# Attention and a two-layer MLP on one core: loading the first units' queries without their zeros, in two half-height parts

## The chip, the cores and the metric

The kernel runs on one core of a Trainium2 chip. The metric is the device time of one execution in microseconds (us), as the median of repeated runs; a smaller time is better. One execution was also taken by the hardware profiler, and the profile and the trace of this text are from it.

## The reference

There are 4 sequences of 768 positions, 8 heads of 64 elements, and 8 memory keys and values per head. Attention is chunked: a chunk of 32 queries sees 16 positions to its left, its own 32, 8 to its right, and the memory. All is in 32-bit floats.

```python
for c in range(nc):                                   # chunks of 32
    k_full = concat(mem_k, k[l_start:r_end])          # v_full likewise
    scores = scale * q_c @ k_full.T
    a = exp(scores - max(scores))
    out[c] = (a / (sum(a) + 1e-9)) @ v_full
x = out.transpose(0, 2, 1, 3).reshape(3072, 512)
h = x @ w_in                                          # 512 -> 2048
g = maximum(h, 0) + alpha * minimum(h, 0)
result = g @ w_out                                    # 2048 -> 512
```

## The kernel before

**Units.** Attention is cut into 32 units: a half of a sequence (384 positions) times a pair of heads, the two heads' 64 elements making the 128 rows of a tile. Units 0 to 7 (two halves with four pairs each) go a way of their own, `windows` (L496), because the MLP can't start before them; the later 24 go through `scores`, `weights` and `turn`, between matmuls of the MLP.

**The first units.** What unit u needs lies in one of four tiles `early` (L212), unit u + 4 coming after unit u in the same tile. A tile has three parts: queries, keys, values. The query part has 768 columns: for each of the 12 chunks 64 columns, 32 of the one head and 32 of the other. Only the rows of a column's own head hold queries; the other 64 rows hold zeros, so that one matmul with 128 rows gives the scores of both heads. These zeros are written on the host (`qd` in `_layout`, L927) and come with the load. `load_first` (L485) issues two DMAs a unit: queries and keys in one (656 KB), values in another (256 KB).

For each of these units `windows` then plans:

- TensorE: `score_products` (L300) loads 64 columns of queries as weights and streams 64 keys through them, 12 times (24 matmuls in the trace, since a 32-bit product is issued as two). The scores stand in one of two PSUM banks, `s_ps`, by the parity of u. In units 0 to 2 a few idle matmuls stand ahead of it (`stir`, L295).
- VectorE: `top` (L502, a memset and a maximum), `less` (L511, subtract it), then ScalarE `exps`, VectorE `total` (L519) and `inverse`, GpSimd `scale` (L526, into `ew`), TensorE `turn` (L541, six transposes), ScalarE `keep`, TensorE `values` (L553), and `split` (L465), which writes the two parts `xh` and `xl` that the MLP takes.

**The MLP.** Weights come by `load_w` (L594), 512 KB a DMA, and are rebuilt on ScalarE and VectorE (`decode_part`, L613) into two parts. `up` (L718, tile `h_ps`) and `down` (L747, tile `o_ps`) are the matmuls that fill nearly all of TensorE's time. The last four weight tiles lie where the `early` tiles lay.

**The order of the work.** Every step is given to a planner (`Plan`, L123) with its engine, a cost, what it reads and writes, and a due time (`rest`). `send` (L143) plays the steps with these costs: of the steps that could run next on an engine it takes the one with the longest way behind it, and issues it. A load's consumers are ready `LAND` (2.3) after the load's cost on SP has passed; `SHIFT` adds to or takes from the priority of ten single steps, by their number in the order of planning. Each engine then runs its own list in that order. All loads are issued from SP's queue.

Of the kernel before, what the change touches and what calls it, by code (L numbers as in the profile page):

```python
# [18 lines left out]
P = 128  # L19
B, H, S, D = 4, 8, 768, 64  # L20
NM = 8
CH, LEFT, RIGHT = 32, 16, 8
# [3 lines left out]
NJ = TQ // CH  # L26
TK = LEFT + TQ + RIGHT
BT = 384
NHALF = B * S // BT
NT = BT // TQ  # L30
NPAIR = H // 2
# [36 lines left out]
NKT = TK + 2 * NM  # L68
STARTS = (0, LEFT + CH // 2, TK - 2 * CH + 2 * NM)

PE, DVE, ACT, POOL, SP = "PE", "DVE", "ACT", "POOL", "SP"

HOP, LAND, FOLLOW = 0.07, 2.3, 0.1

# [31 lines left out]
NWIN, NSET = 2 * NPAIR, 4  # L108

STARTS_WIN = (0, 2 * LEFT, NKT - KW)  # L110
NQ = NT * NJ * 2 * CH
NV = NT * 2 * D
# [4 lines left out]
GATHER_ACT, HIGH_ACT = range(2, 14), 24  # L117


SHIFT = {5: -7.5, 7: -3.1, 9: -1.3, 10: 4.5, 11: 6.7, 64: 3.3, 65: -2.4, 80: -3.2, 113: -3.6, 172: 8.5}  # L120


class Plan:  # L123
# [19 lines left out]
    def send(self):  # L143
# [6 lines left out]
        for n in reversed(range(len(self.steps))):  # L150
            engine, cost, _, _, rest = self.steps[n]
            behind[n] = max(rest, cost + max((behind[m] + lag[engine] for m in users[n]), default=0.0))
        for n, more in SHIFT.items():
            behind[n] += more
# [27 lines left out]
def body(ctx: ExitStack, tc: tile.TileContext, qvw, kw, first, w_in, w_out, alpha, out):  # L182
    nc = tc.nc
# [22 lines left out]
    qk = [const.tile([P, BT + NT * NKT], F32, name=f"qk{i}") for i in range(NKB)]  # L206
# [4 lines left out]

    early = [wps[NF - NSET + i, 0].tile([P, NQ + NT * NKT + NV], F32, name="early", tag="w") for i in range(NSET)]  # L212
    ews = [turned.tile([P, 2, NJ, P], F32, name=f"ew{i}", tag=f"pt{i}") for i in range(NPT)]
    nc.gpsimd.memset(eye, 0.0)
    nc.gpsimd.affine_select(out=eye, in_=eye, compare_op=ALU.not_equal, fill=1.0, base=0, pattern=[[-1, P]],
                            channel_multiplier=1)
# [11 lines left out]
    step = plan.add  # L228
# [20 lines left out]
    def rest(place):  # L249
        wide = NNARROW * NF  # L250
        return (len(ORDER) - max(place, wide)) * WIDE_PAIR + max(wide - place, 0) * PAIR

    def begins(u):

        return u // NPAIR if u < NWIN else BEGIN[(u - NWIN) // 2]

    def due(u, later=0):

        return rest(begins(u) + later + (5.5 if u >= FIRST_FRONT else 0))
# [35 lines left out]
    def stir(t, num):  # L295

        for _ in range(num):
            nc.tensor.matmul(out=t, lhsT=busy[:, :P], rhs=busy, start=True, stop=True)

    def score_products(u):  # L300
        blk, pr = divmod(u, NPAIR)
        st = state[u]
        s_ps = ps_s.tile([P, 512], F32, name="s_ps", tag=f"s{u % 2}")
        stir(s_ps, STIR[0] if u == 0 else STIR[1] if u < 3 else STIR[2])
        st["s"] = s_ps[:, :2 * NJ * KW].rearrange("p (n k) -> p n k", k=KW)
        t = early[u % NSET]
        q = t[:, :NQ].rearrange("p (c x) -> p c x", c=NT * NJ)
        keys = t[:, NQ:NQ + NT * NKT].rearrange("p (t k) -> p t k", t=NT)
        for n in range(2 * NJ):
            for i in range(2):  # L310
                t, j = n // NJ * 2 + i, n % NJ
                nc.tensor.matmul(  # L312
                    out=st["s"][i * 2 * CH:(i + 1) * 2 * CH, n],
                    lhsT=q[:, t * NJ + j],
                    rhs=keys[:, t, STARTS_WIN[j]:STARTS_WIN[j] + KW],
                    start=True, stop=True,
                )
# [167 lines left out]
    def load_first(u):  # L485
        blk, pr = divmod(u, NPAIR)
        t = early[u % NSET]

        def load(lo, hi):
            nc.sync.dma_start(out=t[:, lo:hi], in_=first[blk, pr, :, lo:hi])  # L490

        state[u] = {}
        step(SP, 1.6, partial(load, 0, NQ + NT * NKT), writes=[("qk", u % NSET)], rest=due(u))
        step(SP, 0.78, partial(load, NQ + NT * NKT, NQ + NT * NKT + NV), writes=[("fv", u % NSET)], rest=due(u))

    def windows(u):  # L496

        st = state[u]
        sk, tks, ak = ("s", u % 2), [("o", 0), ("o", 1)], ("o", 2) if u % 2 else "a"
# [53 lines left out]
        def values():  # L553
# [3 lines left out]
            for t in range(NT):  # L557
                for h2 in range(2):
# [4 lines left out]
                        start=True, stop=True,  # L563
                    )

        step(PE, 1.33 if u < 3 else 0.8, partial(score_products, u), reads=[("qk", u % NSET)], writes=[sk], rest=due(u))
        step(DVE, 0.66, top, writes=[sk, ("mx", u % 3)])
        step(DVE, 0.55, less, reads=[sk, ("mx", u % 3)], writes=e_keys(u))
        step(ACT, 0.52, exps, writes=e_keys(u))
# [24 lines left out]
    def load_w(f):  # L594
        def load(i):
            k, j = ((f, i), 0) if f < NAPART else ((f, 0), i)
            if k not in raw:
                raw[k] = wps[k].tile([P, 2 if f >= NAPART else 1, DM, 2], I32, name="w_t", tag="w")
            nc.sync.dma_start(out=raw[k][:, j].rearrange("p m b -> p (m b)"), in_=srcs[i][f])  # L599

        i = f - NF + NSET
        after = [("qk", i), ("fv", i)] if i >= 0 else []
        for i in range(2):
            step(SP, 1.31, partial(load, i), writes=[("r", f, i)] + after, rest=rest(place_of(f)))

    def place_of(f):
        return PLACE[0, f]
# [229 lines left out]
    def unit_begins(u):  # L837
        if u < NWIN:
            windows(u)
        else:  # L840
            if u % 2 == 0:
                scores([u, u + 1])
        if u < NWIN and u + NSET < NWIN:
            load_first(u + NSET)
        elif u >= NWIN - NKB and u + NKB < NU:
            load_unit(u + NKB)

    for u in range(NSET):
        load_first(u)
        if u == 1:  # L850
            step(SP, 0.6, partial(nc.sync.dma_start, out=al, in_=alpha), writes=["al"])
            step(DVE, 0.1, partial(nc.vector.tensor_scalar, out=rise, in0=al, scalar1=-1.0, scalar2=1.0, op0=ALU.mult,
                                    op1=ALU.add), reads=["al"], writes=["rise"])
    for f in range(NF - NSET):
        load_w(f)
# [3 lines left out]
    for f in range(NF - NSET, NF):  # L859
        load_w(f)  # L860
# [49 lines left out]
def _layout(q, k, v, mem_k, mem_v, moe_w_in, moe_w_out, moe_alpha):  # L910
    import numpy as np

    nh = S // BT
    qT = q.reshape(B, NPAIR, 2, nh, BT, D).transpose(0, 3, 1, 2, 5, 4)
    pad = ((0, 0), (0, 0), (LEFT, RIGHT), (0, 0))
    kp, vp = np.pad(k, pad), np.pad(v, pad)

    def keys(x, mem, s, *spans):
        return np.concatenate([mem if p is None else x[:, :, s + LEFT + p[0]:s + LEFT + p[1]] for p in spans], axis=2)

    kwin = np.stack([keys(kp, mem_k, t * TQ, (-16, 16), None, (16, 72), None, (72, 104)) for t in range(S // TQ)],
                    axis=2)
    kwin = kwin.reshape(B, NPAIR, 2, nh, NT, NKT, D).transpose(0, 3, 1, 2, 6, 4, 5)
    vwin = np.stack([keys(vp, mem_v, t * TQ, (-16, 16), None, (16, 104)) for t in range(S // TQ)], axis=2)
    vwin = vwin.reshape(B, NPAIR, 2, nh, NT, P, D).transpose(0, 3, 1, 5, 4, 2, 6)
    nwin = NWIN // NPAIR
    qd = np.zeros((nwin, NPAIR, 2, D, NT * NJ, 2, CH), q.dtype)  # L927
    for h in range(2):
        qd[:, :, h, :, :, h] = qT.reshape(NHALF, NPAIR, 2, D, NT * NJ, CH)[:nwin, :, h]
    kfirst = np.stack([keys(kp, mem_k, t * TQ, (-16, 16), None, (16, 104), None) for t in range(S // TQ)], axis=2)  # L930
    kfirst = kfirst.reshape(B, NPAIR, 2, nh, NT, NKT, D).transpose(0, 3, 1, 2, 6, 4, 5)
    kfirst = kfirst.reshape(NHALF, NPAIR, P, NT * NKT)[:nwin]
    vparts = vwin.reshape(NHALF, NPAIR, P, NV)
    return dict(
        qvw=np.concatenate([qT.reshape(NHALF, NPAIR, P, BT), vparts], axis=3),
        kw=np.ascontiguousarray(kwin).reshape(NHALF, NPAIR, P, NT, NKT),
        first=np.concatenate([qd.reshape(nwin, NPAIR, P, NQ), kfirst, vparts[:nwin]], axis=3),
        w_in=np.ascontiguousarray(moe_w_in.reshape(NK, P, NF, P).transpose(2, 1, 0, 3)
                                  ).reshape(NF, P, NK * P).view(np.int64),
        w_out=np.ascontiguousarray(moe_w_out.reshape(NF, P, DM)).view(np.int64),  # L940
        alpha=np.ascontiguousarray(moe_alpha.reshape(NF, P).T),
    )
# [15 lines left out]
```

## Time and profile before

| | |
|---|---|
| median of 3 runs | 598.65 us (598.43 to 599.91) |
| the profiled execution | 598.74 us |
| its span, first to last instruction | 596.8 us |
| TensorE matmul busy | 588.1 us (99%) |
| VectorE busy | 387.1 us (65%) |
| ScalarE busy | 210.9 us (35%) |
| GpSimd busy | 37.9 us (6%) |
| mean granted TensorE clock | 1.000 |

In the profile PE is TensorE's matmuls, PEld its weight loads, DVE VectorE, ACT ScalarE, POOL GpSimd, and SPq the queue of SyncE, which issues DMAs. Times in the views are us from the first instruction. A row of the timeline gives start, busy time, engine, line, operation, the written and the read tiles, the shape and a count; in square brackets stands the idle time ahead of it and what ended it. The chain is the work that ended last, followed back from the last instruction. A time between the span and the execution's 598.74 us lies around the program, outside the views.

### The profile page before, as it was taken

How to read it: one execution, taken by the hardware profiler on the slowest of the kernel's cores; microseconds unless marked ns; L12 is line 12 of the kernel's file. 1: busy time of each engine (PE TensorE's matmuls, PEld its weight loads, DVE VectorE, ACT ScalarE, POOL GpSimd, SP SyncE). 2: the span in 40 equal slices, each digit the busy share in tenths (PEclk: the TensorE clock that was granted, in tenths of full speed). 3: DMA queues.
4: the chain of work that ended last, by engine and by line, in shares of the span. 5: the costliest groups of instructions: out<-in, count | busy, mean ns of one | idle time of the engine just before them, and what ended most of it. 6: DMA issues, size and time to landing. Idle time of an engine off the chain costs nothing.

```text
span 596.8 us, 10948 instructions
## 1 busy us (share of the span) xinstructions
PE 588.1 (99%) x4412; PEld 504.9 (85%) x4412; DVE 387.1 (65%) x904; ACT 210.9 (35%) x580; POOL 37.9 (6%) x61
## 2 busy tenths in 40 slices
PE   7999999999999999999999999999999999999997
PEld 4789989888998989989898888888888888888886
DVE  5888889887958768695895852861862771530530
ACT  3788887635122504423233302302400411210201
POOL 3510000010001101010010100100100100000000
PEclk9999999999999999999999999999999999999999
DMA  8999600222040312503304003003101000000001
GB/s 328 351 400 407 246 0 1 66 65 89 2 153 2 100 33 69 152 3 100 100 1 154 1 1 100 2 0 112 60 1 36 0 1 36 36 1 0 1 1 70
DMA packets 21075, 48.95 MB, mean 82 GB/s; under 512 B 2464, under 2 KB 5792, under 8 KB 21024
## 3 DMA queue, kind: packets, MB, share of 16 engines
q1 hardware_dynamic: 20880, 48.12, 22.8%
q8 instruction: 34, 0.56, 0.4%
q14 instruction: 17, 0.14, 0.1%
q10 hardware_dynamic: 144, 0.13, 0.1%
HBM read 41.95 MB, written 6.29 MB: 81 GB/s over the span
## 4 chain that ended last, share of the span: by engine, by line
PE 96%; DMA 3%; SPq 0%; ACT 0%; issue 0%; ACTq 0%
PE h_ps L723 45%; PE o_ps L753 44%; PE a_ps L438 3%; DMA early<-first 3%; PE s_ps L337 2%; PE a_ps L559 1%; PE o_ps L546 0%; PE s_ps L312 0%; SPq L490 0%; SPq L599 0%; ACT o_t L810 0%; ACTq L810 0%
## 5 line engine op out<-in xcount | busy, mean ns | idle before, releaser
L723 PE MATMUL h_ps<-xh,w 128*128 128x384 f32 (+1 forms) x896 | 248.7, 358 | 0.0
L723 PEld LDWEIGHTS h_ps<-xh,w 128*128 128x128 f32 x896 | 164.9, 188 | 16.0
L753 PE MATMUL o_ps<-w,gh 128*128 128x512 f32 x528 | 162.7, 389 | 0.0
L723 PE MATMUL h_ps<-xl,w 128*128 128x384 f32 (+1 forms) x448 | 162.6, 363 | 0.0
L732 ACT ACTIVATE g<-h_ps 128x384 f32<-128x384 f32 (+1 forms) x112 | 60.4, 540 | 195.3 <-PE h_ps L723 129.8
L735 DVE SCALAR_TENSOR_TENSOR g<-g,rise,h_ps 128x384 f32<-128x384 f32 (+1 forms) x112 | 74.7, 668 | 74.8 <-ACT g L732 74.1
L753 PEld LDWEIGHTS o_ps<-w,gh 128*128 128x128 f32 x528 | 99.1, 188 | 20.5
L413 DVE STREAM_TRANSPOSE pt<-e 32x64 f32<-32x64 f32 (+1 forms) x336 | 99.3, 300 | 7.4 <-POOL e L392 2.0
L753 PE MATMUL o_ps<-w,gl 128*128 128x512 f32 x264 | 102.8, 389 | 0.0
L723 PEld LDWEIGHTS h_ps<-xl,w 128*128 128x128 f32 x448 | 84.1, 188 | 10.2
L753 PE MATMUL o_ps<-w,xh 128*128 128x512 f32 x240 | 74.8, 393 | 0.0
L753 PEld LDWEIGHTS o_ps<-w,gl 128*128 128x128 f32 x264 | 49.6, 188 | 10.2
L477 DVE TENSOR_TENSOR xl<-a_ps,xh 128x384 fp32r<-128x384 f32 x32 | 17.6, 552 | 59.7 <-ACT xh L474 59.0
L753 PEld LDWEIGHTS o_ps<-w,xh 128*128 128x128 f32 x240 | 45.0, 188 | 8.9
L392 POOL TENSOR_TENSOR e<-e,den 128x384 f32<-128x384 f32 x24 | 22.8, 948 | 419.6 <-DVE den L389 270.0
L474 ACT CAST xh<-a_ps 128x384 fp32r<-128x384 f32 x32 | 15.0, 482 | 95.5 <-PE a_ps L438 93.7
L741 DVE CAST gh<-g 128x512 fp32r<-128x512 f32 (+1 forms) x72 | 28.8, 401 | 30.6 <-PE o_ps L753 28.2
L745 DVE TENSOR_TENSOR gl<-g,gh 128x512 fp32r<-128x512 f32 (+1 forms) x72 | 46.6, 648 | 1.7
L371 ACT ACTIVATE e<-s_ps,mx 128x64 f32<-128x64 f32 x144 | 43.4, 318 | 11.0 <-DVE mx L363 11.0
L753 PE MATMUL o_ps<-w,xl 128*128 128x512 f32 x120 | 46.8, 390 | 0.0
L371 ACT ACTIVATION_READ_ACCUMULATOR e<-s_ps,mx 128x1 f32 x144 | 30.4, 211 | 0.0
L810 ACT COPY o_t<-o_ps 128x512 f32<-128x512 f32 x21 | 12.2, 591 | 44.6 <-PE o_ps L753 44.2
(57 smaller groups left out, 376.4 us busy)
## 6 DMA issues: line engine op xcount, KB each, us to landing
w_t<-w_in SPq DMA_DIRECT2D x16, 512.0 KB, 10.2
w_t<-w_out SPq DMA_DIRECT2D x16, 512.0 KB, 10.2
qk<-kw SPq DMA_DIRECT2D x24, 272.0 KB, 4.2
v_t<-qvw SPq DMA_DIRECT2D x24, 256.0 KB, 2.8
out<-o_t SPq DMA_DIRECT2D x23, 256.0 KB, 2.1
early<-first SPq DMA_DIRECT2D x8, 656.0 KB, 7.2
qk<-qvw SPq DMA_DIRECT2D x24, 192.0 KB, 4.5
early<-first SPq DMA_DIRECT2D x8, 256.0 KB, 7.1
```

The source lines that it names most:

```text
L371: nc.scalar.activation(out=st["e"][:, i], in_=st["s"][h2][:, n], func=AF.Exp, scale=SCALE, bias=d["mx"][:, u - us[0], n, h2:h2 + 1], accum ...
L392: nc.gpsimd.tensor_tensor(out=st["e"], in0=st["e"], in1=st["den"].broadcast_to([P, NJ * 2, KW]), op=ALU.mult)
L413: nc.vector.transpose(out=pts[u % NPT][quad * CH:(quad + 1) * CH, j, t0:t0 + n1 - n0].rearrange("p t h q -> p (t h) q"), in_=(st["e"], zer ...
L438: nc.tensor.matmul(out=st["a"][h2 * D:(h2 + 1) * D, t * TQ:(t + 1) * TQ], lhsT=st["v"][:, t, h2, :], rhs=pts[u % NPT][:, :, t, h2, :], sta ...
L474: nc.scalar.copy(out=ring[k][0][:, cols], in_=st["a"][:, :BT])
L477: nc.vector.tensor_tensor(out=ring[k][1][:, cols], in0=st["a"][:, :BT], in1=ring[k][0][:, cols].bitcast(F32), op=ALU.subtract)
L723: nc.tensor.matmul(out=h["ps"][:, :n_cols], lhsT=ws[f, 0][:, wk, k * P:(k + 1) * P], rhs=parts(blk, k)[1](xk), start=(k == 0 and n == 0), ...
L732: nc.scalar.activation(out=h["g"], in_=h["ps"][:, :n_cols], func=AF.Relu, scale=-1.0)
L735: nc.vector.scalar_tensor_tensor(out=h["g"], in0=h["g"], scalar=rise[:, f:f + 1], in1=h["ps"][:, :n_cols], op0=ALU.mult, op1=ALU.add)
L741: copy(out=h["gh"], in_=h["g"])
L745: nc.vector.tensor_tensor(out=h["gl"], in0=h["g"], in1=h["gh"].bitcast(F32), op=ALU.subtract)
L753: nc.tensor.matmul(out=o_ps[tt], lhsT=h[gk][:, tt * P:(tt + 1) * P], rhs=ws[f, 1][:, wk], start=(f == first_f and i == 0), stop=(f == last ...
```

## The change

It touches the first eight units' loads and two constants of the planner.

- **Queries without zeros.** The host array `first` now holds only queries (384 columns) and keys (544 columns). The kernel zeroes the other half of each query part once per `early` tile, with eight VectorE memsets of 64 rows by 384 columns, issued right behind the memset of `busy`.
- **Four DMAs a unit in place of two:** keys (272 KB, 128 rows), the one head's queries (96 KB, rows 0 to 63, columns 0 to 383), the other head's (96 KB, rows 64 to 127, columns 384 to 767), and values (256 KB, now read from `qvw`). The planner's costs for them are 0.7, 0.26, 0.26 and 0.67, where they were 1.6 and 0.78. `score_products` reads three planned results in place of one.
- **Interleaved.** A chunk's 64 query columns now lie 12 elements (48 bytes) apart in place of next to each other, so that the 32 of the one head and the 32 of the other still have one stride.
- **Planner.** `LAND` is 3.1 in place of 2.3. Eight units with two more steps each shift the numbers of the later steps by up to 16, and `SHIFT` has ten other entries: by the new numbers they are the second part of unit 3's queries (16), its values' load (17), the load of the first `w_in` (18), steps of units 1, 2, 3, 5 and 6 (71 `values`, 82 `total`, 106 `keep`, 131 `exps`, 143 `top`), `ends` of the first `w_in` (187), and `high` of the second `hidden` step (212).

```diff
-HOP, LAND, FOLLOW = 0.07, 2.3, 0.1
+HOP, LAND, FOLLOW = 0.07, 3.1, 0.1
-SHIFT = {5: -7.5, 7: -3.1, 9: -1.3, 10: 4.5, 11: 6.7, 64: 3.3, 65: -2.4, 80: -3.2, 113: -3.6, 172: 8.5}
+SHIFT = {16: -3.7, 17: -9.5, 18: 2.8, 71: 6.4, 82: 7.0, 106: -6.8, 131: 6.6, 143: 9.9, 187: 8.4, 212: 7.9}
...
+    for t in early:
+        for h2 in range(2):
+            nc.vector.memset(t[h2 * D:(h2 + 1) * D, (1 - h2) * BT:(2 - h2) * BT], 0.0)
...
-        q = t[:, :NQ].rearrange("p (c x) -> p c x", c=NT * NJ)
+        q = t[:, :NQ].rearrange("p (x c) -> p c x", c=NT * NJ)
...
-        def load(lo, hi):
-            nc.sync.dma_start(out=t[:, lo:hi], in_=first[blk, pr, :, lo:hi])
+        def load_q(h2):
+            rows = slice(h2 * D, (h2 + 1) * D)
+            nc.sync.dma_start(out=t[rows, h2 * BT:(h2 + 1) * BT], in_=first[blk, pr, rows, :BT])
+
+        def load(x, lo):
+            nc.sync.dma_start(out=t[:, lo:lo + x.shape[-1]], in_=x)
...
-        step(SP, 1.6, partial(load, 0, NQ + NT * NKT), writes=[("qk", u % NSET)], rest=due(u))
-        step(SP, 0.78, partial(load, NQ + NT * NKT, NQ + NT * NKT + NV), writes=[("fv", u % NSET)], rest=due(u))
+        step(SP, 0.7, partial(load, first[blk, pr, :, BT:], NQ), writes=[("fk", u % NSET)], rest=due(u))
+        for h2 in range(2):
+            step(SP, 0.26, partial(load_q, h2), writes=[("fq", u % NSET, h2)], rest=due(u))
+        step(SP, 0.67, partial(load, qvw[blk, pr, :, BT:], NQ + NT * NKT), writes=[("fv", u % NSET)], rest=due(u))
...
-        step(PE, 1.33 if u < 3 else 0.8, partial(score_products, u), reads=[("qk", u % NSET)], writes=[sk], rest=due(u))
+        step(PE, 1.33 if u < 3 else 0.8, partial(score_products, u), reads=[("fk", u % NSET), ("fq", u % NSET, 0), ("fq", u % NSET, 1)], writes=[sk],
+             rest=due(u))
...
-        after = [("qk", i), ("fv", i)] if i >= 0 else []
+        after = [("fk", i), ("fq", i, 0), ("fq", i, 1), ("fv", i)] if i >= 0 else []
...
-    qd = np.zeros((nwin, NPAIR, 2, D, NT * NJ, 2, CH), q.dtype)
-    for h in range(2):
-        qd[:, :, h, :, :, h] = qT.reshape(NHALF, NPAIR, 2, D, NT * NJ, CH)[:nwin, :, h]
+    qfirst = qT.reshape(NHALF, NPAIR, P, NT * NJ, CH)[:nwin].swapaxes(3, 4)
...
-        first=np.concatenate([qd.reshape(nwin, NPAIR, P, NQ), kfirst, vparts[:nwin]], axis=3),
+        first=np.concatenate([qfirst.reshape(nwin, NPAIR, P, BT), kfirst], axis=3),
```

## The prediction

> **What bounds the kernel now.** I read the page first: its shares, its slices and its chain.
>
> ```profile
> span 596.8 us, 10948 instructions
> PE 588.1 (99%) x4412; PEld 504.9 (85%) x4412; DVE 387.1 (65%) x904; ACT 210.9 (35%) x580; POOL 37.9 (6%) x61
> ...
> DMA  8999600222040312503304003003101000000001
> ...
> PE 96%; DMA 3%; SPq 0%; ACT 0%; issue 0%; ACTq 0%
> ```
>
> TensorE is busy for 588.1 of 596.8 us, so all that any change of loads can win lies in the 8.7 us in which it is not. The DMA digits are full only in the first slices (15 us each). The chain in order of time shows where the 3% of DMA lie:
>
> ```profile
> 2.11 7.87 DMA early<-first
> 9.97 0.14 issue
> ...
> 12.21 9.57 DMA early<-first
> 21.78 0.04 issue
> 21.83 0.92 PE s_ps L312 x24
> ...
> 571.38 21.77 PE o_ps L753 x96
> ```
>
> From 21.83 on the chain is TensorE without a gap. So I listed TensorE alone over the start:
>
> ```profile
> 1.46 3.59 PE L298 MATMUL s_ps<-busy 128*128 128x512 bf16 x8 [1.46 <-DVE warm L224]
> 4.98 1.40 PE L312 MATMUL s_ps<-early 128*64 128x64 f32 x24
> 6.31 0.60 PE L298 MATMUL s_ps<-busy 128*128 128x512 bf16 x2
> 6.84 0.92 PE L312 MATMUL s_ps<-early 128*64 128x64 f32 x24
> 7.78 0.60 PE L298 MATMUL s_ps<-busy 128*128 128x512 bf16 x2
> 8.36 0.92 PE L312 MATMUL s_ps<-early 128*64 128x64 f32 x24
> 10.11 0.92 PE L312 MATMUL s_ps<-early 128*64 128x64 f32 x24 [0.83 <-DMA early<-first]
> ...
> 12.70 0.44 PE L546 MATMUL o_ps<-eye,ew 128*128 128x128 f32 x2 [0.87 <-POOL ew L534]
> 13.62 0.66 PE L546 MATMUL o_ps<-eye,ew 128*128 128x128 f32 x4 [0.48 <-POOL ew L538]
> 14.32 0.92 PE L312 MATMUL s_ps<-early 128*64 128x64 f32 x24
> 15.91 0.92 PE L312 MATMUL s_ps<-early 128*64 128x64 f32 x24 [0.67 <-DMA early<-first]
> ...
> 19.44 1.16 PE L546 MATMUL o_ps<-eye,ew 128*128 128x128 f32 x6 [0.34 <-POOL ew L534]
> ...
> 21.83 0.92 PE L312 MATMUL s_ps<-early 128*64 128x64 f32 x24 [0.23 <-DMA early<-first]
> ```
>
> The rows of L312 with x24 are the units' score steps, in the order of their run (the seventh, which waits for no load, is left out). Waits for loads stand ahead of the fourth, the sixth and the last, whose load is the chain's that landed at 21.78. That makes 0.83 + 0.67 + 0.23 = 1.73 us; waits for GpSimd's `ew` make 0.87 + 0.48 + 0.34 = 1.69. The 1.46 us at the start and the tail after 571.38 + 21.77 = 593.15 are touched by no edit. All gaps that the change can close are thus about 3.4 us, 0.6% of the time. A measurement of this kernel can tell about 0.3%, 1.8 us, from no change: more than the three load waits together.
>
> VectorE is the engine beside it. I listed its rows over the same stretch:
>
> ```profile
> 6.46 0.07 DVE L505 MEMSET s_ps<- 64x16 f32 x1 [5.06 <-PE s_ps L312]
> ...
> 8.89 0.55 DVE L513 TENSOR_TENSOR e<-s_ps,mx 128x384 f32<-128x384 f32 x1
> ...
> 11.10 0.07 DVE L505 MEMSET s_ps<- 64x16 f32 x1 [0.43 <-PE s_ps L312]
> ...
> 16.92 0.07 DVE L507 MEMSET s_ps<- 64x8 f32 x1 [1.23 <-PE s_ps L312]
> ...
> 22.83 0.07 DVE L507 MEMSET s_ps<- 64x8 f32 x1 [0.30 <-PE s_ps L312]
> ```
>
> It waits 0.43 + 1.23 + 0.30 = 1.96 us behind the same three score steps, and has nearly no other gap there. So it has room for the 1.73 us, and little room for more: it is next in line.
>
> **The change, part by part.**
>
> *Fewer bytes.* A unit's scores need 656 KB (671,744 B) before and 272 + 2 x 96 = 464 KB (475,136 B) after; values stay at 256 KB. The rate of this stage and the first landing:
>
> ```profile
> 5.00:10.00 5.00, 4.27 (x77) 3.02 (x76) 3.27 (x10) 1.05 (x2) 0.28 (x1) 1.00 1.02 407
> ```
>
> ```profile
> L490 SPq DMA_DIRECT2D early<-first x16: 327/398/612, 0.7 to 25.1; - x16
> ...
> DMA to landing us min/median/max: 3.0/7.2/9.8
> ```
>
> At 407 GB/s the 196,608 B saved are 0.48 us a unit, 3.9 us over eight. The fourth unit's load, which landed at 9.97, would land at 9.97 - 4 x 0.48 = 8.0 by bytes. Issuing bounds it too: twelve DMAs at 0.398 us from 0.74 end at 5.5, and the shortest landing of 3.0 us gives 8.5. Either is before the PSUM bank is free: this step writes the bank that the second unit's `less` reads until 8.89 + 0.55 = 9.44. So the fourth score step goes at about 9.5 in place of 10.11: 0.6 of the 0.83 us. For the sixth the bytes of the five or six loads ahead of it are worth 2.4 us or more, over its wait of 0.67, and for the last 3.8 over 0.23; both waits go whole. Sum: 0.6 + 0.67 + 0.23 = 1.5 us. What is late next is VectorE and, through it, `ew`. The first three units win nothing: their score steps follow the eight `busy` matmuls and the two pairs without a wait.
>
> *Sixteen more DMAs on SP's queue.* 16 x 0.398 = 6.4 us more of issuing within the first 25 us. I take it at nothing: the first twelve are issued in 4.8 us and carry 1.9 MB, 398 GB/s, about the rate at which they move. If this cover is gone, rival four has the price. The planner's 0.26 for the small ones is below 0.398, so its clock for SP is early; `LAND` at 3.1 against 2.3 takes some of that back.
>
> *Eight memsets on VectorE.* The nearest rows:
>
> ```profile
> 0.91 0.48 DVE L205 MEMSET busy<- 128x512 bf16 x1 [0.91 <-PEq L949]
> ...
> 1.32 1.41 POOL L222 MEMSET ew<- 128x768 f32 x2
> ```
>
> 384 columns at VectorE's 512 in 0.48 are 0.36 us, at GpSimd's 1536 in 1.41 0.35; at most 0.48: eight take 2.8 to 3.8 us from 1.39 on. They lie in VectorE's 5.06 us of idle time before 6.46, ended at 5.2 at the latest; the first unit needs only two of them, by 2.4, before its 4.98. Nothing, and without that cover up to 3.8 us. The memset of `warm` is queued behind them, and its ScalarE step; ScalarE's next work is the first `exps`, after VectorE's 6.46. A gain is excluded.
>
> *Query columns 48 bytes apart.* No row shows TensorE reading with a stride. The nearest are ScalarE's, which reads 32-bit words 8 bytes apart (L622), packed (L646), and 16-bit words both read and written 8 bytes apart (L630):
>
> ```profile
> L630 ACT COPY w_t<-w_t 128x512 int16<-128x512 int16 x14 | 19.5, 1390 | 0.1
> ...
> L622 ACT ACTIVATE a<-w_t 128x512 f32<-128x512 f32 x4 | 2.7, 674 | 1.8 <-DMA w_t<-w_in 1.5 <-DMA w_t<-w_out 0.3
> L646 ACT CAST w<-a 128x512 fp32r<-128x512 f32 x4 | 2.5, 619 | 0.3 <-DVE a L638 0.3
> ```
>
> ```profile
> 6.84 0.78 PEld L312 LDWEIGHTS s_ps<-early 128*64 128x64 f32 x24 [0.42 <-DMA early<-first]
> ```
>
> So a read through a stride costs 674/619 = 1.09 times, the far bound is 1390/619 = 2.25 times. On 24 weight loads of 0.78 us that is +0.07 to +0.97 us a unit. At 0.07 they stay under the 0.92 us of the 24 matmuls, so nothing to 0.55 us over eight units; nearest is L622, a 32-bit read alone, and I take 0.2 us in all. A gain is excluded, since packed columns can't be slower.
>
> *Waits, LAND, SHIFT.* The score step now waits for three landings and two memsets; queued behind it on TensorE are the `turn` and `values` of earlier units, which now wait less. The new order of steps can't be read from a trace of the old one: bounds are the 1.69 us of waits for `ew` won, or as much added. I take nothing. After 22 us TensorE has no gap to win; the weights behind these loads come up to 3.9 us sooner, and no TensorE row waits for them.
>
> Sum against the profiled 598.74: - 1.5 + 0.2 = 597.44. The median is 0.09 us below that execution: **597.4**.
>
> **The rivals.**
>
> *One: 64 rows move at half the rate.* Every load in this trace has 128 rows, so nothing here speaks against it. Then a unit's two query parts cost like 384 KB, with 528 KB beside them: 912 KB, exactly as before. The waits stay as they are, 598.65; between a little won where the keys come first and half a microsecond of issuing added, the time is 598.3 to 599.2. [...] Chance 0.22.
>
> *Two: strided weight loads bind (slower).* If a weight load takes twice as long, a step's loads go from 0.78 to 1.56 us and the step from 0.92 to about 1.6: 8 x 0.68 = 5.4 us. The remaining gaps take up about half, since three steps stand ahead of any gap: + 2.7, or **601.4**. By the far bound, 8 x 0.97 = 7.8, it is 603. It decides from about 0.45 us a step, weight loads of 1.37 us; below, it only eats the gain. For it: the matmuls hide just 0.14 us. Against: L622. [...] Chance 0.16.
>
> *Three: the new order closes waits for `ew` as well.* Of 1.69 us some two thirds go on top: 597.4 - 1.1 = 596.3, and 595.7 with all. For it: earlier scores let VectorE choose freely. Against: VectorE's own gaps there are 1.96 us in all. Chance 0.20.
>
> *Four: SP's queue runs dry.* SP's queue waits for landings of loads that it issued earlier, and at one stop the stream thins:
>
> ```profile
> SPq L599 <- DMA w_t<-w_out: 10.2, 10, 1.6
> SPq L490 <- DMA early<-first: 8.9, 5, 3.2
> ```
>
> ```profile
> 10.00:11.00 1.00, 0.89 (x25) 0.85 (x25) 0.67 (x2) 0.00 (x0) 0.84 (x3) 1.00 0.99 215
> ```
>
> If only so many DMAs can be under way, and each is smaller, less lies ahead when SP stands at a wait for TensorE. Two more such dips, at 215 of 407 GB/s half a microsecond each, with the issuing behind them, take most of the 1.5 us back or more: 598.4 to 599.7. Chance 0.07.
>
> **How the numbers follow.** The forecast has 0.35; its own range is 596.6 (no cost of the stride and some `ew`) to 598.2 (the stride at 0.55 and half of the sixth step's wait). Faster than 596.85: all but 0.02 of rival three and 0.13 of the forecast, 0.31. Slower than 600.45: rival two but for its mild end, 0.13, and 0.04 of the others with a wait that the new order adds, 0.17. Within: 0.52. The range from 595.9 to 601.2 leaves out 0.05 below and 0.11 above.
>
> **What would show it.** Right: no DMA releaser ahead of L312 from the fourth step on; the fourth near 9.5; VectorE's 1.23 gone; L312's x24 still 0.92 to 1.0; the last score step about 1.5 us sooner. Rival one: a unit's landings still 1.65 us apart. Two: PEld rows of L312 at 1.4 or more. Three: rows of L546 without a GpSimd releaser. Four: windows under 300 GB/s between 5 and 20. The forecast is wrong if gaps of TensorE appear after 25 us, or if the `busy` matmuls start later than 1.46.

## The result, and the profile after

| | before | after |
|---|---|---|
| median | 598.64 us | 606.77 us |
| profiled execution | 598.74 us | 607.00 us |
| its span | 596.8 us | 605.1 us |
| TensorE busy | 588.1 us | 594.8 us |
| TensorE not busy in the span | 8.7 us | 10.3 us |

The changed kernel is slower: 1.013 times the time before, 95% interval 1.0113 to 1.0146, outside the predicted range. The two spans differ by 8.3 us: 6.7 of them are more busy time of TensorE, 1.6 more idle time. So the page first, with the granted clock and the DMA's slices:

```profile
span 605.1 us, 10988 instructions
PE 594.8 (98%) x4412; PEld 512.2 (85%) x4412; DVE 390.4 (65%) x912; ACT 211.7 (35%) x580; POOL 36.6 (6%) x61
...
PEclk9799999999999999999999999999999999999999
DMA  8999800022112303223122101102200000100001
```

The count of matmuls is the same, 4412, yet they take 6.7 us more, and one slice has a clock of 7 tenths. TensorE's own list over the start (one row for each run of instructions; the idle time before it in brackets) shows both, and a wait:

```profile
5.37 1.85 PE L315 MATMUL s_ps<-early 128*64 128x64 f32 x24 [0.32 <-DVE early L216]
...
7.69 1.84 PE L315 MATMUL s_ps<-early 128*64 128x64 f32 x24
...
10.00 1.84 PE L315 MATMUL s_ps<-early 128*64 128x64 f32 x24
...
17.75 1.89 PE L315 MATMUL s_ps<-early 128*64 128x64 f32 x24 [4.44 <-DMA early<-first]
19.58 1.54 PE L555 MATMUL o_ps<-eye,ew 128*128 128x128 f32 x6
```

A score step takes 1.84 to 1.89 us where it took 0.92, at a granted clock of 1.00 (7.69, 10.00) as at 0.50 (17.75). The fourth starts at 17.75 in place of 10.11. The weight loads of the second step, which took 0.78 us in the kernel before, show the sign that the prediction named for its rival two (1.4 or more):

```profile
7.68 1.71 PEld L315 LDWEIGHTS s_ps<-early 128*64 128x64 f32 x24 [0.42 <-DVE s_ps L514]
```

The whole group of score matmuls, and the rate in the window that the prediction used:

```profile
L315 PE MATMUL s_ps<-early 128*64 128x64 f32 x192 | 14.5, 310 | 4.8 <-DMA early<-first 4.4 <-DVE early L216 0.3
```

```profile
5.00:10.00 5.00, 4.68 (x54) 3.68 (x53) 1.93 (x7) 0.73 (x2) 0.00 (x0) 1.00 0.85 233
```

233 GB/s in place of 407, the DMA engines busy for 0.85 of the window. And the clock in the wait (the value ahead of the DMA's share):

```profile
14.00:15.00 1.00, 0.00 (x0) 0.00 (x0) 0.97 (x4) 0.52 (x2) 0.27 (x1) 1.00 1.09 300
15.00:16.00 1.00, 0.00 (x0) 0.00 (x0) 1.00 (x3) 0.49 (x1) 1.00 (x2) 0.71 1.09 223
16.00:17.00 1.00, 0.00 (x0) 0.00 (x0) 0.62 (x2) 0.65 (x2) 0.47 (x2) 0.50 1.07 227
```

About two microseconds into the idle time the granted clock falls to 0.50, and the transposes at 19.58 take 1.54 us, where the same six take 0.87 at a clock of 1.00 (24.15 in this list, not shown).

What was late is read from the chain that ended last (start, duration, what):

```profile
10.55 0.59 SPq L494
...
11.18 6.44 DMA early<-first
...
17.75 1.89 PE s_ps L315 x24
```

The load that released the fourth step was the one issued from 10.55, and it took 6.44 us.

SP's own list shows how long the issuing of one unit takes, its keys (L497) and its two query parts (L494), up to the next unit's keys:

```profile
2.39 0.59 SPq L497 DMA_DIRECT2D early<-first  x1
3.02 1.10 SPq L494 DMA_DIRECT2D early<-first  x2
4.16 0.59 SPq L497 DMA_DIRECT2D early<-first  x1
```

That is 4.16 - 2.39 = 1.77 us for three loads, where the prediction had 3 x 0.398 = 1.19. The 475,136 B of a unit in 1.77 us are 268 GB/s, an estimate of the most that this issuing lets through.

The theory from here: three edits cost something of their own, the 48-byte step on TensorE, the 64-row loads on the DMA stream, and the new order, in which SP issues the second part of unit 3's queries behind the first weights' load and unit 4's loads (entry 16 of `SHIFT`). The rivals: the long steps come from the clock or the loads, and the late loads from issuing more of them.

### The profile page after: what moved, and what is told of

Its sections match the earlier page's. It is cut to its first block, busy times and chain, and to the rows that moved or that the text cites. A ratio compares the mean times of both kernels' runs of the same rounds, so it can differ in the third digit from the quotient of the medians.

```text
span 605.1 us, 10988 instructions
## 1 busy us (share of the span) xinstructions
PE 594.8 (98%) x4412; PEld 512.2 (85%) x4412; DVE 390.4 (65%) x912; ACT 211.7 (35%) x580; POOL 36.6 (6%) x61
## 4 chain that ended last, share of the span: by engine, by line
PE 96%; DMA 2%; SPq 1%; issue 0%; ACT 0%; ACTq 0%
PE h_ps L733 44%; PE o_ps L763 43%; PE a_ps L441 3%; PE s_ps L340 2%; DMA early<-first 2%; PE s_ps L315 1%; PE a_ps L568 1%; PE o_ps L555 1%; SPq L494 1%; SPq L497 0%; ACT o_t L820 0%; ACTq L820 0%
## 5 line engine op out<-in xcount | busy, mean ns | idle before, releaser
L416 DVE STREAM_TRANSPOSE pt<-e 32x192 f32<-32x192 f32 (+1 forms) x336 | 99.3, 300 | 7.5 <-POOL e L395 2.0
L733 PEld LDWEIGHTS h_ps<-xl,w 128*128 128x128 f32 x448 | 84.1, 188 | 10.3
```

Source lines behind the costliest of these rows:

```text
L416: nc.vector.transpose(out=pts[u % NPT][quad * CH:(quad + 1) * CH, j, t0:t0 + n1 - n0].rearrange("p t h q -> p (t h) q"), in_=(st["e"], zer ...
L733: nc.tensor.matmul(out=h["ps"][:, :n_cols], lhsT=ws[f, 0][:, wk, k * P:(k + 1) * P], rhs=parts(blk, k)[1](xk), start=(k == 0 and n == 0), ...
```

## The experiments

Each time stands with the median of the kernel before on the same chip. Ratios are to the kernel before. What an edit wins or loses is the difference of two medians; the kernel before itself lies between 598.64 and 599.20 us on these chips, so such a difference is uncertain by some 0.6 us. e1, e3, e6, e9 and e14 leave out the right queries or mix the heads: they show what a part costs and are no versions to use.

**One part undone.** `e1_packed`:

```diff
-        q = t[:, :NQ].rearrange("p (x c) -> p c x", c=NT * NJ)
+        q = t[:, :NQ].rearrange("p (c x) -> p c x", c=NT * NJ)
```

> The changed kernel, but the score products take 64 query columns that lie next to each other, from the same interleaved data: the queries that a product multiplies are the wrong ones, the loads, their order and all counts are the same. Theory (the 48-byte step itself doubles the weight loads): the score step falls from 1.85 to about 0.92 us; the three steps ahead of the 4.44 us wait only lengthen that wait, the five behind it win 0.93 each, so about 602 us in place of 606.8. Rival (the steps are long for another reason, the lower clock or loads writing the tile at the same time): the score steps stay at 1.85 and the time at 606 to 607.

603.21 us (before: 599.20), ratio 1.0041 to 1.0085. The steps are 0.92 us where nothing else holds them; the fourth still waits 4.76 us for its load and the clock still falls (mean 0.70 over 10 to 20 us). The 48-byte step alone makes the score steps long: the rival falls. Undoing it wins 3.6 of the 8.1 us, since the steps ahead of the wait were free. One thing more changes here: with packed columns the first 12 matmuls of the fourth step need only the first part of the queries and run ahead of the wait (at 11.99), so a small part of the 3.6 us may be this and not the step.

`e3_full_rows`:

```diff
-            rows = slice(h2 * D, (h2 + 1) * D)
-            nc.sync.dma_start(out=t[rows, h2 * BT:(h2 + 1) * BT], in_=first[blk, pr, rows, :BT])
+            cols = slice(h2 * BT // 2, (h2 + 1) * BT // 2)
+            nc.sync.dma_start(out=t[:, cols], in_=first[blk, pr, :, cols])
...
-            nc.vector.memset(t[h2 * D:(h2 + 1) * D, (1 - h2) * BT:(2 - h2) * BT], 0.0)
+            nc.vector.memset(t[h2 * D:(h2 + 1) * D, BT:2 * BT], 0.0)
```

> The changed kernel with the two query loads of a unit cut the other way: 128 rows by 192 columns in place of 64 rows by 384, 96 KB each, same number and order, step of 48 bytes kept. The queries of both heads then stand in the same columns and the zeros beside them, so scores are mixed over heads. Theory (64 rows move at about half the rate): over 1 to 9 us the rate rises from about 230 to 300 GB/s or more, the fourth score step's load lands 2 to 3 us sooner than 17.6, its wait of 4.44 falls to 1.5 to 2.5, and the time to 603.5 to 605. Rival (the rows don't matter, issuing four DMAs a unit does): landings and time stay, 606 to 607.5.

603.71 us (before: 599.20), ratio 1.0047 to 1.0094: 3.1 us won. The wait falls to 1.28 us, but the rate over 1 to 9 us only to 245 GB/s from 214, less than expected. Issuing is faster too: SP takes 0.43 us for one of these loads (e3's row at 5.43 us), and 0.508 us (median) for one of 64 rows (the row below, of the changed kernel). A unit's three loads are issued in 1.42 us in place of 1.77, and the first eleven in 5.1 in place of 6.3. How much of the 3.1 us is issuing and how much the rate of 64 rows isn't separated here.

```profile
L494 SPq DMA_DIRECT2D early<-first x16: 465/508/606, 1.2 to 20.6; - x16
```

In e3's list the first step and the memsets show whom that step waits for:

```profile
1.42 3.91 DVE L216 MEMSET early<- 64x384 f32 x8
...
5.21 1.89 PE L315 MATMUL s_ps<-early 128*64 128x64 f32 x24 [0.16 <-DMA early<-first]
...
14.69 1.89 PE L315 MATMUL s_ps<-early 128*64 128x64 f32 x24 [1.28 <-DMA early<-first]
```

`e4_no_shift16`:

```diff
-SHIFT = {16: -3.7, 17: -9.5, 18: 2.8, 71: 6.4, 82: 7.0, 106: -6.8, 131: 6.6, 143: 9.9, 187: 8.4, 212: 7.9}
+SHIFT = {17: -9.5, 18: 2.8, 71: 6.4, 82: 7.0, 106: -6.8, 131: 6.6, 143: 9.9, 187: 8.4, 212: 7.9}
```

> The changed kernel without the entry 16 of SHIFT, so that the second part of unit 3's queries is issued right behind the first, ahead of the first weights and of the loads of units 4 and 5. Theory (this order makes TensorE's 4.44 us wait, and the wait the low clock behind it): the fourth score step goes at 12 to 13 us in place of 17.75, no granted clock of 0.5 follows, and the time is 602.5 to 604.5; the score steps stay at 1.85. Rival (the loads as such are late, whatever the order): a wait as long stands at the fourth or fifth score step, 606 to 607.

604.14 us (before: 599.20), ratio 1.0057 to 1.0099: 2.6 us won. The third and fourth steps run one behind the other (48 matmuls from 10.09), and a wait of 1.66 us moves to the fifth:

```profile
10.09 3.46 PE L315 MATMUL s_ps<-early 128*64 128x64 f32 x48
13.48 0.88 PE L555 MATMUL o_ps<-eye,ew 128*128 128x128 f32 x6
16.02 1.83 PE L315 MATMUL s_ps<-early 128*64 128x64 f32 x24 [1.66 <-DMA early<-first]
17.78 0.88 PE L555 MATMUL o_ps<-eye,ew 128*128 128x128 f32 x6
```

Here the transposes behind the wait take 0.88 us, not 1.54: after 1.66 us of idle time no slow clock shows in them (1.00 over 14 to 20 us). (In e1 a mean clock of 0.70 over 10 to 20 us and 0.96 over 20 to 30 put the fall to 0.50 at about 14, an estimate: some 1.5 us into its wait, which begins at 12.56. So these runs give no sharp length of idle time.)

**One part alone.** `e2_strided`, the kernel before with the columns 48 bytes apart:

```diff
-        q = t[:, :NQ].rearrange("p (c x) -> p c x", c=NT * NJ)
+        q = t[:, :NQ].rearrange("p (x c) -> p c x", c=NT * NJ)
...
-    qd = np.zeros((nwin, NPAIR, 2, D, NT * NJ, 2, CH), q.dtype)
+    qd = np.zeros((nwin, NPAIR, 2, D, 2, CH, NT * NJ), q.dtype)
     for h in range(2):
-        qd[:, :, h, :, :, h] = qT.reshape(NHALF, NPAIR, 2, D, NT * NJ, CH)[:nwin, :, h]
+        qd[:, :, h, :, h] = qT.reshape(NHALF, NPAIR, 2, D, NT * NJ, CH)[:nwin, :, h].swapaxes(3, 4)
```

> The kernel before, with its own loads, zeros from the host, order and planner constants; only the query columns are laid out 48 bytes apart, and the score products read them so. Theory (step of 48 bytes): score steps of 1.85 us, 7.0 us more of TensorE's time over eight units, of which TensorE's gaps of some 2 to 3 us take up a part: 602.5 to 604 us. Rival: 598.6.

603.05 us (before: 599.20), ratio 1.0041 to 1.008: 3.9 us lost by the step alone; no wait for a load is left in TensorE's list. Two smaller steps, with all else as before; in `e7_step8` pairs of chunks are interleaved, in `e8_step16` (4 in place of 2) fours:

```diff
-        q = t[:, :NQ].rearrange("p (c x) -> p c x", c=NT * NJ)
+        q = t[:, :NQ].rearrange("p (a x c) -> p a c x", a=NT * NJ // 2, c=2)
...
-                    lhsT=q[:, t * NJ + j],
+                    lhsT=q[:, (t * NJ + j) // 2, (t * NJ + j) % 2],
...
-        first=np.concatenate([qd.reshape(nwin, NPAIR, P, NQ), kfirst, vparts[:nwin]], axis=3),
+        first=np.concatenate([qd.reshape(nwin, NPAIR, P, NT * NJ // 2, 2, 2 * CH).swapaxes(4, 5).reshape(nwin, NPAIR, P, NQ), kfirst, vparts[:nwin]], axis=3),
```

> The kernel before with the query columns of two chunks interleaved, so that the 64 columns of a product lie 8 bytes apart; all else as before. [...] Rival (any step costs as much as 48 bytes): 1.84 us and 603.

> The kernel before with the query columns of four chunks interleaved, so that the 64 columns of a product lie 16 bytes apart. [...] Rival (the cost grows with the distance): between 0.92 and 1.84 us, 600 to 602.

598.91 us (ratio 0.999 to 1.0013) and 601.77 us (1.003 to 1.006), before 598.97. The group of score matmuls over the first 60 us, busy time and mean ns, with 8, 16 and 48 bytes:

```profile
L312 PE MATMUL s_ps<-early 128*64 128x64 f32 x192 | 7.9, 235 | 1.9 <-DMA early<-first 1.7
```

```profile
L312 PE MATMUL s_ps<-early 128*64 128x64 f32 x192 | 12.6, 291 | 0.2
```

```profile
L312 PE MATMUL s_ps<-early 128*64 128x64 f32 x192 | 14.1, 301 | 0.1
```

The kernel before has 7.8 and 235. 8 bytes are free, 16 cost most of what 48 do, though not quite all: 12.6 against 14.1. So e8 fell in the range of its rival (the cost grows with the distance, 600 to 602 us); steps between 8 and 16 bytes weren't run.

`e10_rows_halved` and its control `e11_cols_halved` cut the 656 KB load of the kernel before into two, by rows or by columns:

```diff
-            nc.sync.dma_start(out=t[:, lo:hi], in_=first[blk, pr, :, lo:hi])
+            for rows in ([slice(0, D), slice(D, P)] if lo == 0 else [slice(0, P)]):
+                nc.sync.dma_start(out=t[rows, lo:hi], in_=first[blk, pr, rows, lo:hi])
```

```diff
-            nc.sync.dma_start(out=t[:, lo:hi], in_=first[blk, pr, :, lo:hi])
+            for a, b in ([(0, hi // 2), (hi // 2, hi)] if lo == 0 else [(lo, hi)]):
+                nc.sync.dma_start(out=t[:, a:b], in_=first[blk, pr, :, a:b])
```

> The kernel before, order and bytes unchanged, but its load of queries and keys is issued as two DMAs of 64 rows by 1312 columns (328 KB each). Theory (64 rows move at half the rate): over 3 to 9 us about 205 to 230 GB/s in place of 409, the units' landings some 3 us apart in place of 1.65, 604 to 610. Rival (64 rows move as fast as 128, only small transfers are slow): 390 GB/s or more and 598.5 to 599.5.

> The control to e10: the same two DMAs of 328 KB a unit, cut by columns (128 rows by 656 columns each). Theory: 390 GB/s or more and 598.5 to 599.7, since one more issue a unit is hidden. If the number of DMAs were the cause, it would be as slow as e10.

611.66 us (ratio 1.0191 to 1.0233) against 599.72 us (0.9995 to 1.0018), before 598.92. The same bytes in as many DMAs, in the window of 3 to 9 us, by rows and by columns:

```profile
3.00:9.00 6.00, 4.56 (x31) 1.98 (x29) 1.07 (x3) 0.00 (x0) 0.00 (x0) 1.00 1.04 239
```

```profile
3.00:9.00 6.00, 5.53 (x68) 3.13 (x69) 2.27 (x7) 0.53 (x1) 0.00 (x0) 1.00 1.02 386
```

The engines are busy in both (1.04 and 1.02); 64 rows move at 239/386 = 0.62 of the rate. For these loads of 328 KB it is the rows and not the number of DMAs: e11 has eight DMAs more than the kernel before and can't be told from it.

**Parts undone together.** `e6_packed_order` has the edits of e1 and e4, `e9_three_undone` those of e1, e3 and e4.

> The changed kernel with two parts undone: score products take columns next to each other (wrong queries, as in e1_packed), and SHIFT has no entry 16. The 64-row loads, four a unit, stay. Theory (three costs that add up): 606.8 less 3.6 and 2.6, so 600 to 601.5, score steps of 0.92, and waits for loads of 2 to 4 us left. Rival (once two are undone the load side wins what its bytes promise): 597 to 598.5.

> The changed kernel with three parts undone: columns next to each other (wrong queries), no entry 16 of SHIFT, and query loads of 128 rows by 192 columns (heads mixed). Four loads a unit, the memsets, LAND and the other entries of SHIFT stay. Theory (e6 stayed at 604.9 because the 64-row loads alone hold the stage back): rate over 1 to 9 us above 245 GB/s, waits for loads under 1.5 us, 598.5 to 600.5. Rival (what holds it back is the number of loads, eight under way at a time and issued one by one): waits of 3 us or more, 603 to 605.

604.89 us (before 598.97; ratio 1.0086 to 1.012) and 601.53 us (before 598.92; 1.0021 to 1.0067). Both missed what was expected, and e6 is slower than e1 or e4 alone. The gains don't add: with two undone TensorE is through its steps sooner, and waits for the same 64-row loads (2.88 us at the fifth step, and 1.32 for values); behind the wait of 2.88 us the six transposes take 1.54 us (at 16.29; 0.88 in e4 at 17.78), and the profiled run has a mean clock of 0.996 (1.000 in e4). That this makes up the whole difference isn't shown. With three undone a wait of 1.34 us and one of 0.98 for values are left. Open was whether four loads a unit cause them, or the order of `LAND` and `SHIFT`. (In the traces of the kernel before and of the changed one at most eight DMAs are between their issue and their landing at a time.) `e13_land` is the kernel before with `LAND` at 3.1; `e14_two_loads` is e9 with queries and keys in one load:

```diff
-            cols = slice(h2 * BT // 2, (h2 + 1) * BT // 2)
-            nc.sync.dma_start(out=t[:, cols], in_=first[blk, pr, :, cols])
+            pass
...
-            nc.vector.memset(t[h2 * D:(h2 + 1) * D, BT:2 * BT], 0.0)
+            nc.vector.memset(t[h2 * D:(h2 + 1) * D, :BT], 0.0)
...
-        step(SP, 0.7, partial(load, first[blk, pr, :, BT:], NQ), writes=[("fk", u % NSET)], rest=due(u))
+        step(SP, 0.7, partial(load, first[blk, pr], NQ - BT), writes=[("fk", u % NSET)], rest=due(u))
```

> The kernel before with LAND at 3.1 and nothing else changed. Theory (LAND has no part in the loss, the loads' order stays): 598.3 to 599.7. Rival (a later LAND turns the order of steps against the loads): 600.5 or more.

> e9_three_undone with a unit's queries and keys in one load of 128 rows by 928 columns (464 KB), at the place of the keys' load, so that a unit has two loads in place of four; the data is that of dense queries beside zeros, read by the same wrong columns. Theory (what is left of the loss in e9, 2.6 us, comes from issuing four loads a unit with eight under way): 598 to 599.7, waits for loads of 0.5 us or less up to the last unit. Rival (it comes from the order that LAND and the other entries of SHIFT make): 600.5 to 602.

599.14 us (ratio 0.9995 to 1.0016) and 597.87 us (0.9976 to 0.9996), before 598.74. `LAND` alone, in the order of before, does nothing that can be told. With two loads a unit the rest of the loss is gone, and a little is won, more than was expected. Over 3 to 9 us e14's loads move at 374 GB/s and e9's at 287. No score step waits for a load any more, only for VectorE:

```profile
8.94 0.92 PE L315 MATMUL s_ps<-early 128*64 128x64 f32 x24 [0.32 <-DVE den L532]
...
11.36 0.92 PE L315 MATMUL s_ps<-early 128*64 128x64 f32 x24 [0.41 <-DVE e L521]
...
16.48 0.92 PE L315 MATMUL s_ps<-early 128*64 128x64 f32 x24 [0.25 <-DVE e L521]
...
19.31 0.92 PE L315 MATMUL s_ps<-early 128*64 128x64 f32 x24
```

`e16_zeros_order` puts the loads of before, with their zeros, into that order of steps (no memsets):

```diff
+    qd = np.zeros((nwin, NPAIR, 2, D, NT * NJ, 2, CH), q.dtype)
+    for h in range(2):
+        qd[:, :, h, :, :, h] = qT.reshape(NHALF, NPAIR, 2, D, NT * NJ, CH)[:nwin, :, h]
...
-        first=np.concatenate([qfirst.reshape(nwin, NPAIR, P, BT), kfirst], axis=3),
+        first=np.concatenate([qd.reshape(nwin, NPAIR, P, NQ), kfirst], axis=3),
```

> A whole version with the kernel before's loads (queries with zeros and keys in one load of 656 KB, values in another) and its products, but in the order of e14_two_loads (LAND 3.1, its other entries of SHIFT, the same numbers of the steps); no memsets. It differs from e14 in 192 KB a unit, the memsets and what the queries hold. Theory (the saved bytes win the 0.9 us of e14): 598.5 to 600, with waits for loads of 1.5 us or more. Rival (the order wins them): 597.5 to 598.2.

600.29 us (before 598.95; ratio 1.0011 to 1.0029), with waits of 0.80, 1.21 and 0.32 us for loads; three rows of its TensorE list:

```profile
8.62 0.92 PE L312 MATMUL s_ps<-early 128*64 128x64 f32 x24 [0.80 <-DMA early<-first]
...
13.30 0.92 PE L312 MATMUL s_ps<-early 128*64 128x64 f32 x24 [1.21 <-DMA early<-first]
...
20.16 0.56 PE L312 MATMUL s_ps<-early 128*64 128x64 f32 x10 [1.53 <-issue]
```

A little above the range expected, and far from the rival's. So e14's gain is not the order's: that order with all bytes is 1.3 us slower than before. That the saved bytes win it is the reading left, but the wait of 1.53 us that is put down to issuing isn't in e14's list, so that the 2.4 us between e16 and e14 aren't all shown to be the bytes'.

**A whole version with dense queries.** `e5_heads` is the kernel before with dense queries and keys in one load and a product for each head, which needs no zeros; `e12_heads_busy` adds three `busy` matmuls where e5 stood idle; `e15_heads_order` has e5's products with e14's loads and order.

```diff
-                nc.tensor.matmul(
-                    out=st["s"][i * 2 * CH:(i + 1) * 2 * CH, n],
-                    lhsT=q[:, t * NJ + j],
-                    rhs=keys[:, t, STARTS_WIN[j]:STARTS_WIN[j] + KW],
-                    start=True, stop=True,
-                )
+                c = t * NJ + j
+                for h2 in range(2):
+                    rows = slice(h2 * D, (h2 + 1) * D)
+                    nc.tensor.matmul(
+                        out=st["s"][(i * 2 + h2) * CH:(i * 2 + h2 + 1) * CH, n],
+                        lhsT=q[rows, c * CH:(c + 1) * CH],
+                        rhs=keys[rows, t, STARTS_WIN[j]:STARTS_WIN[j] + KW],
+                        start=True, stop=True,
+                    )
```

> The kernel before with dense queries and no zeros at all: queries and keys in one load of 128 rows (464 KB), and every score product cut into one for each head (64 rows, 32 columns next to each other), as the later units have it; planner constants and numbers unchanged. Theory (the bytes were worth having, what cost was the step, the 64 rows and the order): score steps of about 0.6 us, since 96 such matmuls take 1.17 us in the later units, waits for loads of 1.73 us mostly gone, 595.5 to 597.5 us. Rival (VectorE sets the pace of this stage, so earlier loads and shorter score steps win nothing): 598 to 599.5.

> e5_heads with three more busy matmuls where TensorE stood idle: one ahead of the fourth score step, two ahead of the second unit's transposes. Theory (e5 won its loads' waits and lost them to a granted clock of 0.5 at 13.5 to 16.9 us, which followed idle time): clock 0.999 or more in most runs, 597.2 to 598.4, just faster than before. Rival (the low clock has nothing to do with these gaps, or VectorE sets the pace): 599 to 600.2 as e5.

> A whole version that keeps the saved bytes: the loads and the order of e14_two_loads (dense queries and keys in one load of 128 rows, LAND 3.1, SHIFT without entry 16), no memsets, and the products for each head of e5_heads, which need no zeros. Theory (the loads and the order are what won in e14): 597 to 598.3, at or under the kernel before. Rival (the 48 matmuls a step, which left the clock low and TensorE waiting to issue in e5 and e12, cost it again): 599 to 600.5.

599.80 us (before 598.97; ratio 0.9997 to 1.0019), 599.81 us (before 598.92; 0.9992 to 1.0017) and 600.38 us (before 598.83; 1.0013 to 1.0032). None beats the kernel before. The step of 48 matmuls takes 0.87 us, not 0.6. In e12 and e15 a gap of 1.71 and 1.91 us stands on TensorE, which waits for nothing that the profile shows; here e15's:

```profile
19.02 0.38 PE L554 MATMUL o_ps<-eye,ew 128*128 128x128 f32 x2 [1.91 <-issue]
```

In e5 the granted clock is 0.50 over 14 to 16 us, with TensorE at work:

```profile
14.00:15.00 1.00, 1.00 (x29) 0.67 (x31) 1.00 (x4) 1.00 (x3) 0.03 (x1) 0.50 0.93 333
15.00:16.00 1.00, 1.00 (x48) 1.00 (x44) 0.43 (x1) 0.74 (x2) 1.00 (x2) 0.50 1.00 306
```

The added `busy` matmuls of e12 did not keep that time away: in its profile it lies in 20 to 30 us (0.83 there). The runs of e5 and e12 fall apart by their mean granted clock: the eight at 0.999 or more took 597.44 to 599.01 us, the thirteen at 0.996 or 0.997 took 599.36 to 600.60. So what e5 and e12 lose lies in the runs with the low clock; what lowers it isn't shown, and e15 is slow with either clock (599.54 at 1.000). Why TensorE stops to issue isn't settled: these three programs have some 190 more TensorE matmuls, but e16 has the gap too (1.53 us) with as many as before.

## Why the prediction was wrong, point by point

**Query columns 48 bytes apart: the step that failed first.** The prediction took 0.2 us in all, "nearest is L622". The runs show weight loads of 1.71 us in place of 0.78, 0.92 us more a step, near the far bound of 0.97, and 3.9 us for the edit alone (e2). L622 was the wrong neighbour: it reads 8 bytes apart, which costs TensorE nothing either (7.9 us for all score matmuls against 7.8, e7), while the change takes 48, and the cost begins between 8 and 16 bytes (12.6 us, e8). The bound was right, the choice between the bounds was not. A matmul of this group takes 235 ns on average packed and with 8 bytes, 291 with 16 and 301 with 48; why the cost begins where it does no run shows. The size, 1.85/0.92 = 2.0 times a step, comes from the runs.

**Fewer bytes: the rate.** The 0.48 us saved a unit was reckoned at 407 GB/s for every load. Rows of 64 moved at 0.62 of the rate of 128 (239 against 386 GB/s, e10 and e11), so rival one's cause was real. But the half from which it has its 912 KB is shown by no run; at 0.62 a unit's loads cost like 272 + 192/0.62 + 256 = 838 KB, an estimate, and that is less than before. So the rate of 64 rows alone doesn't make these loads late: over 5 to 10 us the DMA engines are busy for 0.85, not 1.02, and issuing and order come on top. With 128 rows in one load (e14) no score step waits for a load; its median is 0.9 us under the kernel before (0.2 to 1.4 by the interval), in the direction of the 1.5 us forecast and short of it.

**Sixteen more DMAs: taken at nothing, wrongly.** The cover was that twelve loads are issued in 4.8 us, 398 GB/s. In the changed kernel the first eleven took 6.3 us (0.73 to 7.04), 1.77 us a unit and thus 268 GB/s, and the twelfth, by the new order, went out at 10.55. Undoing all but the number of loads leaves 601.53 us; two loads a unit give 597.87, 3.7 us less. A part of this is the clock, 0.83 over 20 to 30 us of e9's profile: the one run of e9 with a mean clock of 1.000 took 599.49. Rival four, which put the price of this at 1.0 to 2.3 us, had SP wait for landings; here the time of issuing itself is what the rows show.

**Waits, LAND, SHIFT: taken at nothing.** `LAND` was nothing in the order of before (e13). Entry 16 wasn't: 2.6 us (e4). The other nine entries weren't undone one by one; with `LAND` and the planner's new costs they make the old loads 1.3 us slower (e16). The prediction knew which step entry 16 moves, and that each engine runs its list in order, but didn't follow it through: the fourth score step held back unit 4's, whose query loads, issued from 8.19 us on, landed 6.4 us later (median), at about 15, more than 2 us ahead of 17.75.

**Memsets: right.** They took 378 ns each, as priced, and ended at 5.33 us, 0.1 past the 5.2 allowed. The wait of 0.32 us ahead of the first step is put down to them, but with full rows (e3) the first step starts at 5.21, and its matmuls wait 0.16 us for the load, while the memsets of later units run until 1.42 + 3.91 = 5.33: that step's own zeros were long there.

**How the numbers followed.** Rivals one and two were each priced alone, at 598.3 to 599.2 and 601.4 to 603, as if only one could be true. The causes of both were there, with slower issuing, an order that made the late loads later and a halved clock behind the wait. No sum over them was made, and the upper end of the range fell short by 5.6 us. The two prices together would have reached 604.8, so the sum alone doesn't give 606.77 either: issuing and order had to be in it. The parts undone one by one win 3.6, 3.1 and 2.6 us, more than the 8.1 lost, so no exact share of each is known.

## What to carry to other kernels

Bytes saved by cutting a load into smaller ones of half the rows can be lost again, here at 0.62 of the rate (e10 against e11) and 0.508 us of issuing in place of 0.43 (after against e3): ask of each transfer how many rows it covers and how long its queue takes to issue it before counting its kilobytes. The score weights of this kernel load in the same time packed or 8 bytes apart (6.8 us for all eight steps in both, e7), and at 48 bytes in about double (13.4 us, e2). Rivals that are independent can be true together, so the far end of the range should hold their sum, and where an operation isn't in the trace the distance in kind (8 bytes or 48) tells which row is near.

## What the runs showed of the hardware that was not expected

- Issuing costs SP more for 64 rows: 0.508 us (median) against 0.43 (the row at 5.43 us) for a load of 96 KB (after against e3), and 0.570 against 0.410 in the medians over all first loads of e10 and e11. The first 64-row load, with one load ahead of it, already took 0.55.
- A step of 16 bytes costs a little less than one of 48: 601.77 against 603.05 us (e8 and e2).
- The granted clock fell to 0.50 some two microseconds into a wait of 4.44 us and stayed there for 6.83 us (15.4 to 22.2 by the clock's own record), some 4.5 of them with TensorE at work. In e1 the spell is about as long (0.70 over 10 to 20 us, 0.96 over 20 to 30). A mean of 0.83 over ten microseconds, as in e3 (10 to 20), e9 and e12 (20 to 30), is a spell at 0.50 of some 3.4 us, an estimate, and e5's 0.73, 0.50, 0.50 and 0.56 over 13 to 17 add up to the same. e6 and e15 show it in the mean clock of the profiled run alone (0.996 and 0.997).
- Score steps with the 48-byte step take about as long at a clock of 0.50 (1.89 us at 17.75) as at 1.00 (1.84 at 10.00), and their weight loads 1.74 and 1.70; a packed step, mostly at 0.50, takes 1.46 in place of 0.92 (e1, at 19.63). So the granted clock doesn't set the pace of the 48-byte steps; that reading the weights does is the likely cause and wasn't tested apart.
